# First layer from a step table, with swapped rows in its second stage; stages of the later batches moved

## The chip, the cores and the metric

The kernel runs on one NeuronCore of a Trainium2 chip. TensorE (PE) multiplies matrices into PSUM; VectorE (DVE), ScalarE (ACT) and GpSimd (POOL) work element by element, and only the first two of them read PSUM here; SyncE (SP) issues most of the DMAs, GpSimd the loads of inputs. Each engine works through its own queue in order and waits on semaphores. The metric is the device time of one execution in microseconds.

## The reference

The input `x` is 8 batches of 3008 rows and 256 columns. Each column of a batch is filtered in the frequency domain, and the result goes through two matrices with a leaky ReLU between:

```python
X = np.fft.rfft(x, axis=1)
y = np.fft.irfft(X * (filt_r + 1j * filt_i)[None], n=3008, axis=1)
h = y.reshape(24064, 256) @ w_in          # 256 x 2048
out = np.maximum(0.01 * h, h) @ w_out     # 2048 x 256
```

## The kernel before

3008 is 94 times 32, so the transform is done as two small ones in each direction, four stages of matmuls with constant tables. Stage one (s1) multiplies x by a 94-point table, stage two (s2) by one 32-point table for each of 24 columns of frequencies, then the filter is applied, stage three (sa) goes back over the 32 points and stage four (sb) over the 94. Between stages one and two, and between three and four, the data must be turned so that another index lies on the partitions.

**Batches 1 to 7** turn through DRAM. `s1_group` writes pieces of `dz1`, `t1_load` reads them back as `z1`, `s2_group` multiplies and applies the filter, `sa_group` multiplies and stores to `dz2`, `t2_load` reads `z2`, and `sb_group` makes `yt`, the input of the expert layers. Each stage has 16 or 12 groups per batch. Real and imaginary parts lie in the upper and lower 64 partitions, and the filter is complex. So `s2_group` makes two products on VectorE: p1 with `fa_sb`, which holds the real filter in both halves, and p2 with `fb_sb`, which holds the imaginary one with a changed sign in one half. Two DMAs on SP swap the halves of p2 into p3 (in batch 1 every second group writes p3 swapped, by two half-height operations), and GpSimd adds p1 and p3.

**Batch 0, the first layer,** must be done before any expert matmul and is written out by hand. `first_s1` does stage one; `t1_part` turns by VectorE's 32x32 transpose within SBUF; `first_s2` does stage two, twice 128 columns of data (`hf`), and multiplies by the two filters: on VectorE straight from PSUM, or, with `on_pool`, by a ScalarE copy and GpSimd. `first_sa` needs no swap, since it adds two matmuls, one with the table `inv2` and one with its halves exchanged, `inv2x`. `first_t2` turns again, and `first_sb` makes `yt` in 16 groups, each copied by ScalarE or VectorE (`quad_copy`). The filter is loaded to 64 partitions of `fa_sb` and `fb_sb`; `upper` fills the other 64, on ScalarE for `fa_sb`, on VectorE with the sign turned (`minus`) for `fb_sb`. `keep_warm` puts matmuls on zeros into TensorE's gaps.

**The expert layers** run over 47 chunks of 512 tokens. `moe1` multiplies by `w_in`, 16 pieces of 2 matmuls, with ScalarE's leaky ReLU for every second piece. `plain` multiplies by `w_out` directly (chunks 0 to 3 and the last). `products` does it with seven products of half size instead of eight; for these, VectorE makes sums of the activations (`act_sums`, four per chunk) and of the outputs, and `wt_sums` prepares sums of the weights.

**What orders the work.** After the first layer, everything is put into a heap with a time in *steps* and issued in that order on each engine: `at(time, f)`, or `soon(delay, f)` from inside another item. One chunk of `moe1` is 8 steps. `plan(b, s1, s1_step, s2, s2_step, lag, sb, sb_step, xl, x_step)` gives each group of batch b its time: s2 group g is at s2 + s2_step·g, its sa group `lag` later, and so on. The groups are then sorted, with at least GAP = 0.6 steps between any two. Loads are placed LANDED steps after the last group of the stage that they read, but not before `s2 - 3` or `sb - 3`:

```python
after = when[stage, b, 15 if stage == 1 else 11] + LANDED
at(max(time, after, place.get((stage, c % 4), 0)), f)
```

The step times decide only the order within each queue; on the chip an item runs when its queue reaches it and its semaphores allow.

Of the kernel before, what the change touches and what calls it, by code (L numbers as in the profile page):

```python
# [11 lines left out]
P = 128  # L12
FP16 = mybir.dt.float16
FP32 = mybir.dt.float32
# [5 lines left out]
N1, N2 = 94, 32  # L20
# [6 lines left out]
def _build_np_constants(N):  # L27
# [36 lines left out]
    inv2x = np.concatenate([inv2[64:], inv2[:64]], axis=0)  # L64
    small = np.stack([fwd1, inv2, inv2x], axis=1)
# [8 lines left out]
def kernel(  # L74
# [25 lines left out]
    LANDED = 1.7  # L100
    SUMS = (0.9, 1.9, 2.9, 3.9)
# [11 lines left out]
    small_sb = cpool.tile([P, 3, P], FP16, name="small_sb")  # L113
# [36 lines left out]

    def soon(delay, f):
        at(clock["now"] + delay, f)
# [3 lines left out]
    fwd1, inv2, inv2x = (small_sb[:, i, :] for i in range(3))  # L156
# [11 lines left out]
    def filt_load(dst, src, d0, dn):  # L168

        for q, first, sgn in ((0, 0, 1), (Q, N1, -1)):  # L170
            nc.gpsimd.dma_start(
                dst[q : q + Q, :, ds(d0, dn)],
                bass.AP(tensor=src.tensor, offset=src.offset + first * D + d0,
                        ap=[[N1 * D, N2 // 2], [sgn * NC * D, 2], [sgn * D, NC], [1, dn]]))
# [8 lines left out]
    for hf in range(2):  # L183
        filt_load(fa_sb, filt_r, hf * DH, DH)
        filt_load(fb_sb, filt_i, hf * DH, DH)
        if hf == 0:
            nc.gpsimd.dma_start(f2_sb[:, ts(2, NC // FP), :], f2_d.ap()[2])
# [26 lines left out]
    st1, st2, st1_more = ring(big[2], 0), ring(big[2], 1), ring(big[0], 0)  # L214

    def s1_group(b, g, copy):
        def go():
            ps = bank("pf", 2, D)
            nc.tensor.matmul(ps, fwd1[:N1], x_sb[:N1, ds(2 * g, 2), :], start=True, stop=True)  # L219
            h = g // 2  # L220
            st = st1[h % 4] if b > 1 or h < 4 else st1_more[h % 4]
            copy(st[:, ds(2 * (g % 2), 2), :], ps)  # L222
            if g % 2:
                soon(0.7, lambda: nc.sync.dma_start(dz1[b % 2][ds(4 * h, 4)].rearrange("n p d -> p n d"), st))
        return go

    def t1_load(b, c):
        def go():
            nc.sync.dma_start(z1[c % 4], turned(dz1[b % 2], N2, c))
        return go  # L230

    def t2_load(b, h):
        def go():
            nc.sync.dma_start(z2[h % 4][:K4], turned(dz2[b % 2], NC, h))
        return go
# [11 lines left out]
    def t1_part(b, i, flat=False):  # L247
        def go():
            a = big[(4 * b) % 3][:].bitcast(FP32)[:, ts(i, E4 * Q)].rearrange("p (e n) -> p e n", n=Q)
            o = big[(4 * b + 1) % 3][:].bitcast(FP32)  # L250
            if flat:
                o = o[:, ts(i, E4 * Q)].rearrange("p (e n) -> p e n", n=Q)
            else:
                o = o.rearrange("p (n e) -> p e n", n=Q)[:, ts(i, E4), :]
            nc.vector.transpose(o, a)
        return go


    ys = {}

    def s2_group(b, g):
        def go():
            ps = bank("pf", 2, D)
            for j in range(2):
# [8 lines left out]
            else:  # L273
                nc.vector.tensor_tensor(p2[:], ps, fb, AL.mult)  # L274
                soon(1, lambda: nc.sync.dma_start(p3[0:64], p2[64:P]))
                soon(1, lambda: nc.sync.dma_start(p3[64:P], p2[0:64]))
            nc.vector.tensor_tensor(p1[:], ps, fa, AL.mult)  # L277
            ys[(b, g)] = y1 = ypp.tile([P, 2, D], FP16, tag="y", name=f"y_b{b}_g{g}")
            soon(1.2 if b == 1 and g % 2 == EXG else 3 if b > 1 else 2.6, lambda: nc.gpsimd.tensor_tensor(y1[:], p1[:], p3[:], AL.add))  # L279
        return go  # L280

    def sa_group(b, g):
        def go():
            ps = bank("pf", 2, D)
            nc.tensor.matmul(ps, inv2, ys.pop((b, g))[:], start=True, stop=True)  # L285
            h = g // 2
            nc.scalar.copy(st2[h % 4][:, ds(2 * (g % 2), 2), :], ps)  # L287
            if g % 2:
                soon(0.7, lambda: nc.sync.dma_start(dz2[b % 2][ds(4 * h, 4)].rearrange("k p d -> p k d"), st2[h % 4]))
# [7 lines left out]
    def sb_group(b, g, copy):  # L297
        h, dt = g // 2, g % 2

        def go():  # L300
            ps = bank("pf", 4, N1)
            for j in range(4):
# [6 lines left out]
    two = ("pf", "ph")  # L309
    act, dve = nc.scalar.copy, nc.vector.tensor_copy  # L310

    def first_s1(n0, n, kind, copy):
        ps = bank(kind, n, D)
        for j in range(0, n, 2):
            nc.tensor.matmul(ps[:, ds(j, 2), :], fwd1[:N1], x_sb[:N1, ds(n0 + j, 2), :],
                             start=True, stop=True)
        spread(big[0], n0, ps, copy)
# [4 lines left out]
             for hf in range(2)]  # L322

    def first_s2(hf, c, n, kind, on_pool=False):
        ps = bank(kind, n, DH)
        src = paired(big[1])
        for j in range(n):
            nc.tensor.matmul(ps[:, j, :].rearrange("p (e t) -> p e t", t=2), f2_sb[:, c + j, :],
                             src[:, c + j, ts(hf, DH // 2)], start=True, stop=True)
        fs = [f[:, ds(c, n), ts(hf, DH)] for f in (fa_sb, fb_sb)]  # L330
        y = [prods[hf][:, i, ds(c, n), :] for i in range(2)]
        if on_pool:
            xs = [scrp.tile([P, 4, DH], FP32, tag=f"p{j // 4 + 1}", name=f"fx_h{hf}_c{c + j}")
                  for j in range(0, n, 4)]
            for j, xf in enumerate(xs):
                act(xf[:], ps[:, ts(j, 4), :])
            for i in range(2):
                for j, xf in enumerate(xs):
                    nc.gpsimd.tensor_tensor(y[i][:, ts(j, 4), :], xf[:], fs[i][:, ts(j, 4), :], AL.mult)
        else:  # L340
            for i in range(2):
                nc.vector.tensor_tensor(y[i], ps, fs[i], AL.mult)

    def first_sa(hf, c, n=4):
        y = [prods[hf][:, i, ds(c, n), :] for i in range(2)]
        for j in range(0, n, 4):
            ps = bank("pf", 4, DH)
            for i, m in enumerate((inv2, inv2x)):
                nc.tensor.matmul(ps, m, y[i][:, ds(j, 4), :], start=(i == 0), stop=(i == 1))  # L349
            act(paired(big[2])[:, ds(c + j, 4), ts(hf, DH // 2)],  # L350
                ps.rearrange("p n (t e) -> p n e t", t=2))


    def first_t2(i):
        a = big[2][:].bitcast(FP32)[:, ts(i, E4 * Q)].rearrange("p (e n r) -> p e n r", n=Q // 2, r=2)
        o = big[0][:].bitcast(FP32).rearrange("p (h n e r) -> p h e n r", h=2, n=Q // 2, r=2)
        nc.vector.transpose(o[:, i // 2, ts(i % 2, E4)], a)

    def first_sb(g, copy, kind):
        dt, h = g // 8, g % 8  # L360
        src = big[0][:].rearrange("p (h n e r t) -> p h n r t e", h=2, n=Q // 2, r=2, t=2)
        ps = bank(kind, 4, N1)
        for j in range(4):
            n2 = 4 * h + j
            for t in range(2):
                nc.tensor.matmul(ps[64 * t : 64 * t + 64, j, :], src[:, dt, n2 // 2, n2 % 2, t, :],
                                 i1_sb[:, n2, :], start=True, stop=True)
        quad_copy(h, dt, ps, copy)

    def upper(hf, t, copy):  # L370
        copy(t[64:P, :, ts(hf, DH)], t[0:64, :, ts(hf, DH)])

    def minus(o, i):
        nc.vector.tensor_scalar(o, i, -1.0, None, AL.mult)

# [6 lines left out]
    keep_warm(18)  # L382
    g = 0
    for (n0, nn), fill in zip(first_parts, (4, 3, 1, 14)):
        while nn:
            n = 2 if nn % 4 or n0 >= N2 - 4 else 4
            first_s1(n0, n, two[n // 4], (dve, act)[g % 2])
            n0, nn, g = n0 + n, nn - n, g + 1
        keep_warm(fill)
    t1_part(0, 0, True)(), t1_part(0, 1, True)()  # L390
    upper(0, fa_sb, act), upper(0, fb_sb, minus)
    first_s2(0, 8, 8, "ph", True)
    t1_part(0, 2, True)()
    first_s2(0, 0, 8, "ph")

    nc.vector.memset(i1_sb[:, 0, 0:2], 0.0)
    nc.sync.dma_start(i1_sb[:], i1_d.ap())
    first_s2(0, 16, 4, "pf", True)
    for n0 in (0, N2 // 2):
        x_load(1, n0, N2 // 2)  # L400
    t1_part(0, 3, True)()
    first_s2(0, 20, 4, "pf")
    upper(1, fa_sb, act)
    upper(1, fb_sb, minus)
    keep_warm(4)
    first_s2(1, 8, 8, "ph", True)
    first_s2(1, 0, 8, "ph")
    first_sa(0, 0, 8)
    first_s2(1, 16, 8, "ph")
    nc.gpsimd.dma_start(w_out_sb[:], moe_w_out.rearrange("(ct p) d -> p ct d", p=P))  # L410
    first_sa(0, 20), first_sa(0, 8, 8), first_sa(0, 16)
    first_sa(1, 0, 8)
    keep_warm(3)
    first_t2(0), first_t2(1)
    first_sa(1, 16), first_sa(1, 20), first_sa(1, 8, 8)
    first_t2(2), first_t2(3)
    keep_warm(2)
    for g in range(8):
        first_sb(g, act, two[(g // 2) % 2])
    for g in range(8, 16):  # L420
        first_sb(g, act if g in (10, 12, 14) else dve, two[(g // 2) % 2])
# [44 lines left out]
    def act_sums(ci, step):  # L466
# [3 lines left out]
        nc.vector.tensor_tensor(o, i0, i1, op)  # L470

# [171 lines left out]
```

## Time and profile before

| | |
|---|---|
| three runs | 756.97, 759.53, 760.03 us, median 759.53 |
| profiled execution | 758.15 us, span from the first to the last instruction 756.4 us |
| busy: PE, ACT, DVE, POOL | 740.5, 563.0, 483.1, 165.0 us |
| largest group on PE | L442 (`moe1`), 447.2 us for 1728 matmuls, which overlap |
| first expert matmul | at 38.4 us |
| HBM | 57.48 MB read, 50.33 MB written |

Line numbers are those of the kernel before. A row of the timeline or of a group reads: start, length, engine, line, operation, what it writes and reads, how often, and in brackets the idle time before it with what ended it. A chain of waits is followed back from the last instruction: start, length, what was running or awaited. "PEclk" is the clock granted to TensorE, in tenths of full speed in the page's slices and as a fraction in a table of stretches.

### The profile page before, as it was taken

The page shows a single profiled execution, that of the slowest core. Times are in us where ns is not written, and L with a number is a line of the kernel's source. Part 1 is how long each engine was busy: PE and PEld are TensorE (multiplying, and loading weights), DVE is VectorE, ACT ScalarE, POOL GpSimd, SP SyncE. Part 2 cuts the span into 40 slices and gives each one's busy share as a digit, 9 for nine tenths or more (in the row PEclk, how much of TensorE's full clock was granted, in tenths as well). Part 3 has the DMA queues.
Part 4 walks back from the last instruction along what each step waited for, and adds up shares of the span by engine and source line. Part 5 has one row for each costly group of instructions (what it writes and reads, how often), then busy time and mean ns, then how long its engine had stood idle before and what let it go on. Part 6 is the DMA issues. An engine that isn't in the chain of part 4 may idle for free.

```text
span 756.4 us, 18976 instructions
## 1 busy us (share of the span) xinstructions
PE 740.5 (98%) x7829; PEld 529.5 (70%) x7829; DVE 483.1 (64%) x658; ACT 563.0 (74%) x755; POOL 165.0 (22%) x171
## 2 busy tenths in 40 slices
PE   8899989999999999999999999999999999999998
PEld 4556657677677777877678767787777777777776
DVE  5965525777666685767667666676667766555462
ACT  4876777788778877777778777878777777776663
POOL 4703421332223121221233222212111210000000
PEclk9999999999999999999999999999999999999999
DMA  9997786887985668555665656544554433121012
GB/s 190 245 215 193 172 203 172 197 197 201 223 207 144 142 185 209 145 158 127 188 191 138 163 141 184 145 141 116 154 154 121 119 92 103 57 64 53 29 44 70
DMA packets 119687, 113.29 MB, mean 150 GB/s; under 512 B 16352, under 2 KB 92768, under 8 KB 119408
## 3 DMA queue, kind: packets, MB, share of 16 engines
q1 hardware_dynamic: 104736, 95.59, 42.8%
q0 software_dynamic: 14864, 16.49, 15.7%
q8 instruction: 61, 1.00, 0.6%
q14 instruction: 26, 0.21, 0.1%
HBM read 57.48 MB, written 50.33 MB: 143 GB/s over the span
## 4 chain that ended last, share of the span: by engine, by line
PE 88%; DMA 5%; DVE 3%; ACT 2%; issue 1%; POOL 1%; SPq 0%; DVEq 0%; POOLq 0%; ACTq 0%
PE ph L442 39%; PE pf L493 17%; PE po_ps L493 17%; PE pf L219 3%; PE pf L303 3%; PE pf L265 2%; PE pf L285 2%; DMA p_b_g<-p_b_g 2%; DMA big<-dz 2%; PE po_ps L545 1%; PE pf L545 1%; PE po_ps L379 1%; DMA dz<-big 1%; PE pf L349 1%; POOL y_b_g L279 1%
## 5 line engine op out<-in xcount | busy, mean ns | idle before, releaser
L447 ACT ACTIVATE gt_c<-ph 128x1024 f16<-128x1024 f32 x376 | 385.4, 1025 | 138.1 <-PE ph L442 129.4
L442 PE MATMUL ph<-yt,w_in_sb 128*128 128x512 f16 (+7 forms) x1728 | 447.2, 351 | 0.0
L493 PEld LDWEIGHTS <-gt_c 128*128 128x128 f16 x2688 | 194.3, 98 | 91.6 <-issue 2.8
L279 POOL TENSOR_TENSOR y_b_g<-p_b_g,p_b_g 128x512 f16<-128x512 f32 x84 | 114.0, 1358 | 443.8 <-DMA p_b_g<-p_b_g 309.5
L493 PEld LDWEIGHTS <-big 128*128 128x128 f16 x2016 | 144.8, 98 | 61.8 <-issue 1.1
L442 PEld LDWEIGHTS <-w_in_sb 128*128 128x128 f16 x1728 | 138.1, 98 | 19.7 <-issue 1.0
L274 DVE TENSOR_TENSOR p_b_g<-pf,fb_sb 128x512 f32<-128x512 f32 x78 | 53.7, 689 | 51.8 <-PE pf L265 31.5
L493 PE MATMUL pf<-wt_sb,gt_c 128*128 128x128 f16 x672 | 67.5, 219 | 0.0
L493 PE MATMUL po_ps<-wt_sb,gt_c 128*128 128x128 f16 x672 | 67.4, 219 | 0.0
L222 ACT CAST big<-pf 128x512 f16<-128x512 f32 x100 | 58.2, 583 | 11.9 <-PE pf L219 10.7
L493 PE MATMUL po_ps<-wt_sb,big 128*128 128x128 f16 x672 | 64.8, 219 | 0.0
L493 PE MATMUL pf<-wt_sb,big 128*128 128x128 f16 x672 | 64.0, 219 | 0.0
L493 PE MATMUL po_ps<-w_out_sb,gt_c 128*128 128x128 f16 x672 | 63.9, 219 | 0.0
L493 PE MATMUL pf<-w_out_sb,gt_c 128*128 128x128 f16 x672 | 63.5, 219 | 0.1
L295 ACT CAST yt<-pf 128x376 f16<-128x376 f32 x117 | 55.0, 472 | 9.5 <-PE pf L303 7.2
L277 DVE TENSOR_TENSOR p_b_g<-pf,fa_sb 128x512 f32<-128x512 f32 x84 | 57.2, 681 | 0.2
L287 ACT CAST big<-pf 128x512 f16<-128x512 f32 x84 | 49.1, 584 | 9.6 <-PE pf L285 8.4
L470 DVE TENSOR_TENSOR gt_c<-gt_c 128x2048 f16<-128x2048 f16 x42 | 54.5, 1297 | 1.1
L470 DVE TENSOR_TENSOR big<-gt_c,big 128x2048 f16<-128x2048 f16 x42 | 54.9, 1308 | 0.0
L470 DVE TENSOR_TENSOR big<-big,gt_c 128x2048 f16<-128x2048 f16 x42 | 52.7, 1256 | 0.0
L470 DVE TENSOR_TENSOR big<-gt_c 128x2048 f16<-128x2048 f16 x42 | 52.1, 1241 | 0.2 <-ACT gt_c L447 0.2
L219 PE MATMUL pf<-x_sb,small_sb 94*128 94x512 f16 x112 | 42.7, 381 | 1.1 <-DVE p_b_g L277 0.9
(84 smaller groups left out, 642.4 us busy)
## 6 DMA issues: line engine op xcount, KB each, us to landing
dz<-big SPq DMA_DIRECT2D x98, 256.0 KB
p_b_g<-p_b_g SPq DMA_DIRECT2D x156, 128.0 KB
out_dram<-ost_c_h SPq DMA_DIRECT2D x114, 128.0 KB
big<-dz SPq DMA_DIRECT2D x42, 256.0 KB
big<-dz SPq DMA_DIRECT2D x56, 192.0 KB
x_sb<-in_x_dram POOLq DMA_DIRECT2D x41, 192.0 KB, 4.5
out_dram<-ost_c_t SPq DMA_DIRECT2D x14, 128.0 KB
x_sb<-in_x_dram POOLq DMA_DIRECT2D x2, 768.0 KB, 10.1
```

The source lines that it names most:

```text
L219: nc.tensor.matmul(ps, fwd1[:N1], x_sb[:N1, ds(2 * g, 2), :], start=True, stop=True)
L222: copy(st[:, ds(2 * (g % 2), 2), :], ps)
L274: nc.vector.tensor_tensor(p2[:], ps, fb, AL.mult)
L277: nc.vector.tensor_tensor(p1[:], ps, fa, AL.mult)
L279: soon(1.2 if b == 1 and g % 2 == EXG else 3 if b > 1 else 2.6, lambda: nc.gpsimd.tensor_tensor(y1[:], p1[:], p3[:], AL.add))
L287: nc.scalar.copy(st2[h % 4][:, ds(2 * (g % 2), 2), :], ps)
L295: copy(yv, ps.rearrange("p c a -> p a c"))
L303: nc.tensor.matmul(ps[:, j, :], z2[h % 4][:K4, j, ts(dt, P)], i1_sb[:K4, 4 * h + j, :], start=True, stop=True)
L442: nc.tensor.matmul(ph[:, j, ds(t - ci * CH, e - t)], w_in_sb[:, dt, ts(ct, P)], yt[:, dt, ds(t % N, e - t)], start=(dt == 0), stop=(dt == ...
L447: nc.scalar.activation(gts[ci][:, ds(2 * g, 2), :], ph, AF.Lrelu)
L470: nc.vector.tensor_tensor(o, i0, i1, op)
L493: nc.tensor.matmul(po[:, t], a()[:, c, ts(t, P)], w[:, c, :], start=(c == 0), stop=(c == NCH - 1))
```

## The change

*One filter tensor at first.* The loads put the real filter into partitions 0 to 63 of `fa_sb` and the imaginary one into 64 to 127; `upper` and `minus` are gone. Stage two of the first layer is done twice: once as before (`i` = 0), once with the two 64-column halves of its table exchanged (`i` = 1), each half with a matmul of its own, so that real and imaginary rows come out swapped. Each result is multiplied by the same `fa_sb`, and two new tables `inv2r` and `inv2i` in stage three add what belongs together.

*A table.* The first layer is a list of steps, `FIRST`, each with its PSUM bank and engine; matmuls, copies and products are separate steps. Transposes write a layout in which stage two's moving operand takes 4 bytes in every 8; before, it took 4 in every 128.

*Two token groups.* Of the second half's eight sb groups only (1,1) and (1,0) are in the table. The other six are issued at steps REST among the expert layers (`late_sb`).

*Filter copies later.* At steps 1 to 5, two SBUF-to-SBUF DMAs on SP and two sign changes on VectorE fill `fb_sb` and the lower half of `fa_sb` for the other batches.

*Stages moved.* All numbers of `plan`, LANDED, SUMS and the delays of `soon` are new; the planner now defers a group whose load or sum would not yet have been issued; `need` only asserts an order when the kernel is built.

```diff
-    inv2x = np.concatenate([inv2[64:], inv2[:64]], axis=0)
-    small = np.stack([fwd1, inv2, inv2x], axis=1)
+    inv2r = np.concatenate([inv2[:64], -inv2[:64]], axis=0)
+    inv2i = np.concatenate([inv2[64:], inv2[64:]], axis=0)
+    small = np.stack([fwd1, inv2, inv2r, inv2i], axis=1)
...
-    LANDED = 1.7
-    SUMS = (0.9, 1.9, 2.9, 3.9)
+    LANDED = 2.25
+    SUMS = (0.05, 1.56, 2.78, 3.96)
+    REST = (7.03, 10.88, 12.69, 11.1, 24.89, 21.68)
+    DUE = (3.63, 2.43)
+    LEAD = (3.88, 6.11)
+    AFTER = (0.93, 0.81, 2.51, 2.97, 0.07, 0.45)
+    PLANS = (
+        (0.68, 0.1, 11.58, 1.11, 3.68, 36.48, 2.65, 7.08, 1.57),
+        (11.42, 1.71, 43.13, 2.47, 7.03, 86.57, 2.71, 17.89, 2.06),
+        (39.96, 1.77, 73.73, 3.9, 5.24, 128.81, 2.92, -0.44, 2.56),
+        (64.08, 2.86, 119, 3.89, 7.18, 177.38, 3.01, 9.84, 2.43),
+    )
...
-        filt_load(fa_sb, filt_r, hf * DH, DH)
-        filt_load(fb_sb, filt_i, hf * DH, DH)
+        filt_load(0, filt_r, hf * DH, DH)
+        filt_load(64, filt_i, hf * DH, DH)
...
+            for h in range(2):
+                nc.tensor.matmul(ps[ts(h, 64), j, :].rearrange("p (e t) -> p e t", t=2),
+                                 f2_sb[:, c + j, ts(1 - h, 64)], v, start=True, stop=True)
...
+        s1e 0 12 4 A, s1e 0 24 2 D, s1p 0 20 4 b3, s1e 0 20 4 A, s1p 0 26 2 b0, s1p 0 28 2 b1,
+        s1p 0 30 2 b2, s1e 0 26 2 D, s1e 0 28 2 A, s1e 0 30 2 D, t1 1, t1 0, warm 14, s2p 0 0 4 0 b0,
+        s2p 0 0 4 1 b1, s2p 0 16 4 0 b2, t1 2, t1 3, s2a 0 0 4 0, s2m 0 0 4 0, s2a 0 0 4 1, s2p 0 16 4 1 b0,
...
+        sbp 0 0 b2, sbp 0 3 b4, sbe 0 6 A, sbp 1 1 b3, sbe 0 0 D, sbe 0 2 A, sbp 1 0 b0, sbe 0 3 A,
+        sbe 0 7 A, sbe 1 1 D, sbe 1 0 A
...
+    for g in range(10, 16):
+        at(REST[g - 10], lambda g=g: late_sb(1, g - 8, (act, dve)[g % 2]))
...
-    plan(1, 0.3, 0.55, 12.8, 1.25, 3.3, 37, 2.8, 4, 1.6)
-    plan(2, 13, 1.55, 43.5, 2.6, 5.5, 84.2, 2.8, 13, 2.3)
-    plan(3, 42, 1.75, 75, 3.75, 6, 129, 2.94, 4, 2.94)
-    for b in range(4, B):
-        z = 47 * b
-        plan(b, z - 121, 2.94, z - 69, 3.92, 6.5, z - 11.6, 2.94, 4, 2.94)
+    at(1, lambda: nc.sync.dma_start(fb_sb[0:64], fa_sb[64:P]))
+    for i in range(2):
+        at(1 + i, lambda i=i: nc.vector.tensor_scalar(fb_sb[64:P, ts(i, NC // 2)], fa_sb[64:P, ts(i, NC // 2)],
+                                                      -1.0, None, AL.mult))
+    at(5, lambda: nc.sync.dma_start(fa_sb[64:P], fa_sb[0:64]))
```

In the table, `s1p`, `s2p`, `sap` and `sbp` are the matmuls of a stage, `s1e`, `sae` and `sbe` the copies out of PSUM (A on ScalarE, D on VectorE), `s2d` a product on VectorE, `s2a` with `s2m` a ScalarE copy with a product on GpSimd, `t1` and `t2` the transposes, `warm` the filler.

## The prediction

> **What bounds the kernel now.** I read the page first: busy shares, then the forty slices.
>
> ```profile
> span 756.4 us, 18976 instructions
> ...
> PE 740.5 (98%) x7829; PEld 529.5 (70%) x7829; DVE 483.1 (64%) x658; ACT 563.0 (74%) x755; POOL 165.0 (22%) x171
> ...
> PE   8899989999999999999999999999999999999998
> ...
> PEclk9999999999999999999999999999999999999999
> ```
>
> TensorE is busy all the way, so time can be won in two places only: ahead of the first expert matmul, where a busy PE proves little (part of it is `keep_warm` filler), and in single PE stalls later. The chain of waits supports this: 88% of it is PE, 39% L442 alone. So next the timeline of VectorE in the first layer:
>
> ```profile
> 14.78 2.37 DVE L255 STREAM_TRANSPOSE big<-big 128x1024 f32<-128x1024 f32 x2 [0.22 <-ACT big L243]
> 17.18 0.95 DVE L374 TENSOR_SCALAR fb_sb<-fb_sb 64x3072 f16<-64x3072 f16 x1
> ...
> 33.51 2.37 DVE L357 STREAM_TRANSPOSE big<-big 128x1024 f32<-128x1024 f32 x2 [1.03 <-ACT big L350]
> 36.50 1.00 DVE L295 CAST yt<-pf 128x376 f16<-128x376 f32 x2 [0.61 <-PE pf L366]
> ```
>
> From 14.78 to 35.88 (33.51+2.37) VectorE rests once, 1.03 us before the last transposes, because ScalarE came late. VectorE sets the first layer's end; the first expert matmul (L442) starts at 38.4. The stretches show that PE has slack there:
>
> ```profile
> 20.68:24.10 3.42, 1.41 (x13) 1.22 (x13) 3.39 (x6) 2.35 (x2) 3.42 (x4) 1.00 1.25 216
> 24.10:27.50 3.40, 3.40 (x20) 2.10 (x18) 3.37 (x3) 2.22 (x4) 3.39 (x5) 0.50 1.03 286
> ```
>
> (columns: length, then PE, PEld, DVE, ACT, POOL busy, PE clock, DMA share, GB/s). PE is busy 1.41 of 3.42 us while VectorE has 3.39; in the next stretch PE's clock is half.
>
> For the rest I listed the places where one PE matmul starts later than its predecessor's length allows. From 38.4 to 753 only these exceed 0.3 us: 57.4 (0.73), 68.7 (0.37), 74.2 (0.33), 110.8 (2.11), 142.7 (1.11), 192.8 (0.83), 366.3 (1.90), 452.2 (1.22): 8.6 us. The chain at two of them, cut out:
>
> ```profile
> 52.27 2.60 DMA dz<-big
> ...
> 55.07 3.15 DMA big<-dz
> ...
> 58.27 0.38 PE pf L265 x2
> ```
>
> At 57.4 batch 1's second stage waits for the turn through DRAM: store 2.60, load 3.15. At 110.8 it is the second turn (4.85 and 2.94). At 192.8, 366.3 and 452.2 a swap or load took 6.23, 5.89 and 6.91; at 142.7 a VectorE sum stood in front.
>
> [...] 16 first-layer matmuls of 128 columns (L328), whose moving operand takes 4 bytes in every 128, last 1.92 us, 0.11 each; L493's 128 columns, contiguous, go at 0.39/7=0.056. That 4 bytes in every 8 run at full speed, no row shows. [...] L366's 64-column pairs agree: groups of 16 start at 32.97 and 33.47, 0.50/8=0.06 per pair.
>
> **The change, part by part.** Baseline: span 756.4; that execution timed 758.15, the three timed runs 756.97 to 760.03, median 759.53. I carry the difference over to the median.
>
> *First layer, VectorE.* First stage: the three 1024-element casts of 1.22 become two, with three of 0.68; the last cast (DVE or ACT) ends at 14.28 instead of 14.75: −0.5. The two sign flips (0.95+1.37) leave the path: −2.3. Products: GpSimd took ten of 512 elements (about 1.15 each), now eight; VectorE now has six of 1024 at 1.21 and four of 512 at 0.66, 9.9, against 8.56 in its eight rows before: +1.3. The transposes keep their number and about 1.19 each (L357 has the new output pattern already). The 1.03 rest goes, since ScalarE loses two copies of 2.75 (L371) and takes eight of 0.54 (five before): its last copy before the final transposes comes about 0.3 ahead of them. VectorE's row is then 14.3 + 8×1.19 + 9.9 + 0.06 = 33.8 against 35.88: −2.1. After it, only the two groups (1,0) and (1,1) stand before the first expert matmul instead of eight: their copies, two of 0.54 on VectorE and ScalarE's last ones ending at 35.5, let PE run from about 35.4, 1.6 behind the transposes against 2.5. Sum: **−3.0**.
>
> This needs PE to keep up. Swapped rows add 96 matmuls of 64 columns, in 48 pairs. At 0.056–0.06 each both halves take 96×0.058=5.6 against 48×0.11=5.3; at 0.11 they take 10.6, PE becomes the row that sets the end, and walking it step by step puts the first expert matmul at 37.6–38.0: the gain shrinks to −0.6. [...]
>
> *Moved out.* Six sb groups (`late_sb`) cost PE 0.25 each among full work: **+1.5**. Their copies go to ACT and DVE, which have room (5 to 6 tenths busy).
>
> *Filter copies.* Two SBUF copies on SP and two sign flips on VectorE come back at steps 1 to 5. SP holds its copies behind the filter loads' landings (22.0) and the table load only; the dz1 stores queue behind them. The first flip (0.95) stands on VectorE between two evacuations that PE's stage-one groups need back: **+0.8** (0 to 1.2). The copies' 1.5 MB meet w_out and x: 219 to 271 GB/s there before. The inverse table `i1` is issued at 21.5 (21.7 before, landed 30.09) and needed at 31.4: 0 to +0.7, taken as 0. On GpSimd's queue the loads of batch 1's x and of w_out stand two products earlier, about 3 us ahead of 26.4 and 31.9: they land sooner, nothing waits. The next table, f2, still waits for the last second-stage matmul, at about 27.
>
> *Batch 1's first turn.* LANDED and AFTER put the z1 loads at step 12.88 instead of 11.0. On SP they now stand behind chunk 0's second output store (`t1`), which waits for a VectorE copy that ended at 56.5 before; load at about 57.1, landing 60.3, against PE ready at 57.7 (its group is at 12.91 instead of 12.8). A stall of 2.1 to 2.6 in place of 0.73: **+1.4**. Behind the store on SP wait only those loads and the swaps that follow them; behind the stalled group on PE waits everything, so it counts in full. Bounds: 0.7 (nothing changes) to 3.4, if stores and loads take 0.7 longer.
>
> *Plans.* One step is about 1.85 us here. Last sa to first sb in batch 1: 3.6 → 4.3 steps, −1.2 of the 2.11 at 110.8. Batch 1's sa lags: −0.4. The sums leave step 0.9 for 0.05, away from the product that they delayed at 142.7: −1.0. Batch 2's group 11 gets 5.4 steps instead of 4.8 (+1.1 us): −0.8. Batch 4's group 11 gets 6.24 instead of 6.04 (+0.4) and its swap is queued 0.19 steps earlier: −1.2 of 1.90, the softest term. Batch 6's loads lead by 4.16 instead of 3.0 (+2.1): −1.2. Batch 3's sa groups lose: 4.1 to 6.0 steps instead of 5.0 to 6.65. Measured from s2 to the end of GpSimd's add, its chains took 5.8 to 10.5 us; four of twelve exceed the new lag, by about 2 us less what overlaps: +0.8. Sum: **−5.0**.
>
> Total −3.0+1.5+0.8+1.4−5.0 = −4.3: span 752.1, and 759.53−4.3 = **755.2**.
>
> **Rivals.**
> A (0.56): the sum above; 755.2, own range 751.5–758.5.
> B (0.18), stage two stays at half rate: −0.6 for −3.0, so 757.6. [...]
> C (0.16), the later stalls are jitter of DMAs (3.15 here, 6.91 there) that no plan removes: the −5.0 shrinks to 0, 760.2. For it: batch 4's groups have equal lags, and one of twelve stalled. Against: the stalled groups of batches 1, 2 and 6 had the shortest lags.
> D (0.10), slower: batch 3's second stage, 190 to 280 us, becomes a rhythm of waits: s2, swap, add, sa. Its twelve lags average 5.2 steps. Two neighbouring groups overlap, so a chain of c steps costs about 12(c−5.2)/2 steps. At 8.2 us over A, from chains of about 5.9 steps (11 us), the kernel is slower than before beyond 0.5%; at 12.3 us it ends at 771. For it: 10.0, 10.0 and 10.5 in three groups now. Against: a median of 7.6.
> That the change doesn't do what it says: the filter is loaded with the same bytes and its two other halves are made later, so no transfer is saved, only its place moves; included in A.
>
> **How the numbers follow.** Measurement can tell about 0.5%, 3.8 us, from no change: below 755.7 is faster, above 763.3 slower. A's value lies close under the first bound, and what it may err in (the bounds above) reaches more to the low side, since its losses can be smaller and no stall may remain: 0.48 of its 0.56 I count as faster, with 0.04 of B and 0.02 of C: 0.54. D gives 0.10 slower; 0.36 stays. Low end of the range: A without the flip's 0.8, the turn's 1.4, batch 3's 0.8, and with the rest of the 1.90 and 2.11 won: 755.2−3.0−1.6 = 750.6, put at 750.0. High end: C with the table's 0.7, 761.0; D lies outside.
>
> **What would show it.** Right: VectorE without rest from 14.3 to about 33.8; first L501 matmul near 35; PE clock full from 7 on; L385 rows at about 0.056 per matmul; a PE wait of 2 us on big<-dz near 57; none at 110, 366, 452. Wrong: L385 at 0.11; PE clock halves in several stretches; waits for the add at many groups between 190 and 280; a first L501 later than 37.

## The result, and the profile after

The change made the kernel slower: 766.31 us median of six runs (765.88 to 771.32) against 756.99 (756.16 to 760.03) of the kernel before, ratio 1.0132 with a 95% interval of 1.0096 to 1.0169. The prediction was 755.2, with a range of 750 to 761. The profiled execution of the kernel after timed 766.39.

The page of the kernel after, the lines that answer to those of before:

```profile
span 764.6 us, 19178 instructions
...
PE 742.4 (97%) x7920; PEld 528.9 (69%) x7920; DVE 486.9 (64%) x660; ACT 560.1 (73%) x757; POOL 167.1 (22%) x169
...
PE   8968999999999999999999999999999999999997
...
PEclk9989999999999999999999999999999999999999
```

PE has one slice of 6 tenths, the third (38 to 57 us), with a clock of 8: the loss lies right behind the first layer. Line numbers from here on are those of the kernel after: L501 is `moe1`, L607 `plain`, L247, L296, L318 and L339 the four stages' matmuls, L250 the copy behind L247, L430 the first layer's sb groups, L252 the dz1 stores, L259 the z1 loads, L542 the output stores.

VectorE in the first layer, from the timeline:

```profile
14.39 4.62 DVE L376 STREAM_TRANSPOSE big<-big 128x1024 f32<-128x1024 f32 x4
19.69 2.36 DVE L393 TENSOR_TENSOR prod<-ph,fa_sb 128x1024 f16<-128x1024 f32 x2 [0.67 <-PE ph L385]
...
29.14 4.81 DVE L422 STREAM_TRANSPOSE big<-big 128x1024 f32<-128x1024 f32 x4
33.87 0.51 DVE L329 CAST yt<-pf 128x376 f16<-128x376 f32 x1
```

From 14.39 to 33.95 VectorE rests once, for 0.67 us, and the first L501 starts at 35.17 (38.44 before). The first layer does what was forecast. What PE waited for next, from 34 to 58 us and from 58 to 70:

```profile
PE po_ps L607 <- DMA w_out_sb<-in_moe_w_out_dram: 6.0, 1, 6.0
PE pf L247 <- DVE big L250: 0.8, 1, 0.8
...
PE pf L296 <- DMA big<-dz: 2.7, 1, 2.7
```

(columns: us in total, times, longest). The first `plain` waits 6.0 us for `w_out`, a load that the kernel before had in time. Its issue, from GpSimd's timeline before, and issue to landing, from the chain after:

```profile
31.94 1.22 POOL L410 DMA_DIRECT2D w_out_sb<-in_moe_w_out_dram  x1
```

```profile
28.48 24.61 DMA w_out_sb<-in_moe_w_out_dram
```

Before, the load took 12.6 us and landed at 44.5. The stretches from the wait on:

```profile
46.74:53.12 6.38, 0.38 (x2) 0.10 (x1) 0.68 (x1) 0.90 (x1) 0.00 (x0) 0.79 1.25 255
53.12:57.33 4.21, 4.21 (x15) 2.16 (x15) 0.69 (x1) 1.02 (x1) 0.00 (x0) 0.51 0.96 251
```

PE has 0.38 busy in 6.38, then runs 4.21 us at a clock of 0.51, in which about 2.1 us are lost: the wait of 6.0 costs about 8. A rest of 2.0 us in the kernel before (20.9 to 22.9) has half clock behind it too (0.50 from 24.1 to 27.5). After the 2.7 at the second wait here (65.9 to 68.6) the clock stays full (1.00 from 65.9 to 73), as it does behind a rest of 1.9 in the kernel before (1.00 from 111 to 117). So in these traces the length of a rest alone doesn't tell whether half clock follows. The chain at the second wait:

```profile
63.69 0.43 DVE ost_c_t L612
64.12 0.02 issue
64.14 0.58 SPq L542
...
64.94 3.54 DMA big<-dz
68.48 0.14 issue
68.61 0.38 PE pf L296 x2
```

The z1 loads are issued only after chunk 0's output store (L542), which waited for VectorE's copy of PSUM (L612).

**A ledger.** For every matmul in the trace I took the time to the next one's start and subtracted its own length (0.213 us for 512 columns, as four of L501 at full clock go from start to start: 1.02 us at 35.17, the last one 0.38); the rest is called excess. Before against after: first expert matmul 38.4 to 35.2, −3.3. Matmul work after it 683.0 to 684.9, +1.9 (`late_sb`). Excess up to 58 us 1.2 to 9.7, +8.5; from 58 to 70 us 0.6 to 3.6, +3.0 (of the 1.2, 0.73 is the wait at batch 1's first turn, which the kernel after has behind 58 us; like against like it is +9.2 and +2.3); from 70 to 195 us 8.6 to 7.5, −1.1; from there to the end 20.7 to 19.3, −1.4. Behind the last matmul 3.9 to 4.5, +0.6. The sum is +8.2, the difference of the spans of the two profiled executions; the medians differ by 9.3.

### The profile page after: what moved, and what is told of

The parts are those of the page before. It is cut to its first block, busy times and chain, and to the rows that moved or that the text cites. A ratio compares the mean times of both kernels' runs of the same rounds, so it can differ in the third digit from the quotient of the medians.

```text
span 764.6 us, 19178 instructions
## 1 busy us (share of the span) xinstructions
PE 742.4 (97%) x7920; PEld 528.9 (69%) x7920; DVE 486.9 (64%) x660; ACT 560.1 (73%) x757; POOL 167.1 (22%) x169
## 3 DMA queue, kind: packets, MB, share of 16 engines
q8 instruction: 62, 1.02, 0.6%
## 4 chain that ended last, share of the span: by engine, by line
PE 85%; DMA 10%; POOL 2%; DVE 2%; issue 1%; SPq 0%; ACT 0%; DVEq 0%; POOLq 0%; ACTq 0%
PE ph L501 39%; PE pf L555 17%; PE po_ps L555 17%; DMA w_out_sb<-in_moe_w_out_dram 3%; PE pf L339 3%; PE pf L247 2%; DMA p_b_g<-p_b_g 2%; PE pf L296 2%; PE pf L318 2%; DMA f_sb<-fwd_const 1%; PE po_ps L607 1%; PE pf L607 1%; POOL y_b_g L311 1%; DMA big<-dz 1%; DMA x_sb<-in_x_dram 1%
## 5 line engine op out<-in xcount | busy, mean ns | idle before, releaser
L501 PE MATMUL ph<-yt,w_in_sb 128*128 128x512 f16 (+7 forms) x1728 | 448.2, 352 | 0.5 <-DVE yt L329 0.5
L555 PEld LDWEIGHTS <-gt_c 128*128 128x128 f16 x2688 | 194.6, 98 | 89.1 <-issue 1.1
L311 POOL TENSOR_TENSOR y_b_g<-p_b_g,p_b_g 128x512 f16<-128x512 f32 x84 | 118.1, 1408 | 428.1 <-DMA p_b_g<-p_b_g 307.9
L501 PEld LDWEIGHTS <-w_in_sb 128*128 128x128 f16 x1728 | 137.8, 98 | 22.7 <-issue 3.2
L250 ACT CAST big<-pf 128x512 f16<-128x512 f32 x100 | 58.1, 583 | 12.9 <-PE pf L247 11.1
L529 DVE TENSOR_TENSOR gt_c<-gt_c 128x2048 f16<-128x2048 f16 x42 | 58.0, 1382 | 0.9
L607 PEld LDWEIGHTS <-gt_c 128*128 128x128 f16 x320 | 31.4, 99 | 25.8 <-issue 8.3
```

Source lines behind the costliest of these rows:

```text
L311: ("y", b, g), lambda: nc.gpsimd.tensor_tensor(y1[:], p1[:], p3[:], AL.add)))
L501: nc.tensor.matmul(ph[:, j, ds(t - ci * CH, e - t)], w_in_sb[:, dt, ts(ct, P)], yt[:, dt, ds(t % N, e - t)], start=(dt == 0), stop=(dt == ...
L555: nc.tensor.matmul(po[:, t], a()[:, c, ts(t, P)], w[:, c, :], start=(c == 0), stop=(c == NCH - 1))
L607: nc.tensor.matmul(po, gts[ci][:, ct, ts(tj, P)], w_out_sb[:, ct, :], start=(ct == 0), stop=(ct == NCT - 1))
```

## The experiments

All times are medians of the compared runs; each group of kernels had its own runs of the kernel before (757.18 for the first four kernels, 756.76 for the next four, 756.68 for the last two). The first four take apart what the ledger shows between 35 and 70 us, and the moved stages.

**Filter copies on VectorE instead of by DMA.**

```diff
-    at(1, lambda: nc.sync.dma_start(fb_sb[0:64], fa_sb[64:P]))
+    for i in range(2):
+        at(3 + i, lambda i=i: nc.vector.tensor_copy(fb_sb[0:64, ts(i, NC // 2)], fa_sb[64:P, ts(i, NC // 2)]))
...
-    at(5, lambda: nc.sync.dma_start(fa_sb[64:P], fa_sb[0:64]))
+    for i in range(2):
+        at(5 + i, lambda i=i: nc.vector.tensor_copy(fa_sb[64:P, ts(i, NC // 2)], fa_sb[0:64, ts(i, NC // 2)]))
```

> The changed kernel with its two filter DMAs replaced by four VectorE copies of 64x3072 at steps 3 to 6 (about 0.95 us each, as the sign flips). Theory T: the first filter copy's 12 KB packets held the DMA engines from 37 to 42 us and pushed the w_out load into the time of the dz1 stores; without them w_out lands at 44 to 46 us instead of 53.1, the 6.2 us wait before the first L607 and the half clock after it (about 2.1 us) go, and the kernel takes 757 to 759.5 us (0.988 of the changed kernel, at most 1.5 us given back for the new VectorE copies). Rival R1: w_out is late because the table queues it behind batch 1's x and starts the dz1 stores at 39 us; then it lands after 50 us and the wait stays above 3 us, the kernel above 762.

Measured: 759.37, 7 us under the kernel after. `w_out` landed 17.2 us after its issue at 29.0, at 46.2, hardly later than expected, and no PE wait for it is left. Its waits from 34 to 54 us:

```profile
PE pf L247 <- DVE big L250: 2.1, 4, 0.8
PE pf L430 <- DVE big L250: 0.9, 1, 0.9
```

So theory T holds, and the new VectorE copies cost about 2 us of PE, where at most 1.5 was expected: each, 0.95 us long, stands in front of a copy that frees a PSUM bank.

**The two DMAs later.**

```diff
-    at(1, lambda: nc.sync.dma_start(fb_sb[0:64], fa_sb[64:P]))
+    at(9.5, lambda: nc.sync.dma_start(fb_sb[0:64], fa_sb[64:P]))
...
-    at(5, lambda: nc.sync.dma_start(fa_sb[64:P], fa_sb[0:64]))
+    at(9.6, lambda: nc.sync.dma_start(fa_sb[64:P], fa_sb[0:64]))
```

> The changed kernel with the two filter DMAs at steps 9.5 and 9.6 instead of 1 and 5, nothing else moved. Theory T: w_out lands at 44 to 46 us, no wait before L607; the 1.5 MB of the copies now meet the dz1 stores and z1 loads instead, which delays the first second-stage group of batch 1 by up to 3 us; 758 to 761 us. Rival R1: w_out after 50 us, wait above 3 us, 764 or more.

Measured: 763.34, between the two expectations. `w_out` took 16.6 us and nobody waits for it, as T says, but the price at the other place was far too small. The waits from 34 to 70 us:

```profile
PE pf L296 <- DMA big<-dz: 7.7, 1, 7.7
PE pf L247 <- DVE big L250: 0.8, 1, 0.8
```

The chain at that wait, cut:

```profile
56.60 5.54 DMA dz<-big
...
62.22 2.96 DMA big<-dz
```

The last dz1 store now stands on SP behind both copies and took 5.54 us, the z1 loads came after it, and the wait is 7.7 us instead of 2.7. The second copy overwrites what the first one reads, and SP waited 5.3 us for that: it was issued at 55.0, a microsecond after the first one's last packets, and its packets fill 56 to 60 us; the store's come after them. So this place moves the wait. It doesn't show that no place would do: from 54 to 56 us the DMA engines moved nothing.

**The step numbers of before, on the kernel with VectorE copies (the first one).**

```diff
-    LANDED = 2.25
-    SUMS = (0.05, 1.56, 2.78, 3.96)
+    LANDED = 1.0
+    SUMS = (0.9, 1.9, 2.9, 3.9)
...
-    AFTER = (0.93, 0.81, 2.51, 2.97, 0.07, 0.45)
+    AFTER = (0.7, 1, 3, 2.6, 0.7, 0.5)
...
-        (0.68, 0.1, 11.58, 1.11, 3.68, 36.48, 2.65, 7.08, 1.57),
+        (0.3, 0.55, 12.8, 1.25, 3.3, 37, 2.8, 4, 1.6),
```

(DUE, LEAD and the other three plans likewise; the 1.0 is added to a delay of 0.7.)

> As the kernel with VectorE filter copies, but all step numbers of the stages (plans, sums, landing time, delays) as before the change. Theory P (the moved stages gain, as the prediction summed: about 5.0 us less the first turn's 1.4): slower than the kernel with VectorE copies by 2 to 4.5 us, with stalls again at batch 1's first sb group, at a product behind a VectorE sum, and at the groups 11. Rival C (those stalls are chance of single DMAs): within 1 us of it, stalls of the same total at other groups.

Measured: 758.76, 0.6 us faster than with the new numbers. Theory P's loss didn't come. The time lies within rival C's 1 us, but not for C's reason: the stalls are back at three of P's places (1.19 at batch 1's first sb group, 1.04 behind a VectorE sum at 146, 0.93 at batch 2's group 11), and excess from 70 to 195 us is 9.7 instead of 7.6. What pays for them is seen in the next kernel: in the old numbers batch 1's z1 loads stand ahead of the second output store.

**z1 loads ahead of the store.**

```diff
-            at(t, (t1_load if stage == 1 else t2_load)(b, c))
+            at(t - 0.6 * (stage == b == 1 and c < 4), (t1_load if stage == 1 else t2_load)(b, c))
```

> As the kernel with VectorE filter copies, but batch 1's first four z1 loads stand ahead of chunk 0's second output store on SP; nothing else moves on any queue. Theory Z: the loads start about 1 to 2 us earlier, and the stall before batch 1's first second-stage group, which stands at about 2 to 3 us, shrinks to under 1.2 us; 1.5 to 2.5 us faster than with the VectorE copies alone. Rival: the dz1 stores land too late anyway, the loads start within 0.4 us of before, and the time is the same within 0.5 us.

Measured: 756.04, 3.3 us under the same kernel without it. Theory Z holds and was too low: the wait of 3.1 us became 0.2, and the half clock behind it (64.4 to 67.8 us) went too. The chain to L296 without the change and with it, cut; in the second the waiting DMA is gone:

```profile
58.97 0.55 SPq L542
...
59.75 3.73 DMA big<-dz
63.48 0.14 issue
63.61 0.38 PE pf L296 x2
```

```profile
59.84 0.32 PE po_ps L607 x2
60.16 0.04 issue
60.20 0.38 PE pf L296 x2
60.58 0.43 PE ph L501 x2
```

With this order alike on both sides, the old step numbers (758.76) are 2.7 us slower than the new ones (756.04). So the moved stages are worth −2.7, and the place of one load in SP's queue +3.3: together +0.6.

**Copies and flips in small pieces.** Two kernels, on the one above. In the first all 24 pieces are VectorE's, in the second GpSimd's, at steps 0.1, 0.4 and 0.7 + 1.1·i; the lines that they replace are left out:

```diff
...
+    for i in range(8):
+        w = ts(i, NC // 8)
+        at(1.1 + 1.2 * i, lambda w=w: nc.vector.tensor_scalar(fb_sb[64:P, w], fa_sb[64:P, w], -1.0, None, AL.mult))
+        at(1.5 + 1.2 * i, lambda w=w: nc.vector.tensor_copy(fb_sb[0:64, w], fa_sb[64:P, w]))
+        at(1.9 + 1.2 * i, lambda w=w: nc.vector.tensor_copy(fa_sb[64:P, w], fa_sb[0:64, w]))
```

> As the kernel with VectorE filter copies and z1 loads ahead of the store, but the six filter operations of 64x3072 (0.95 us each) cut into 24 of 64x768 spread over steps 1 to 11. Theory V: the PE waits of 0.98, 0.70, 0.77, 1.03 and 0.35 us between 37 and 48 us come from single long VectorE operations that stand in front of the copies that free the PSUM banks; cut, they fall to under 1.2 us together and the kernel takes 753 to 754.5 us. Rival: VectorE is short of time as a whole there, and the waits keep a sum above 2.5 us: 755.5 to 756.5 us.

Measured: 755.92, no gain; the rival's number. Excess from 35 to 50 us is 3.2 us instead of 4.1. A piece of a quarter took 0.35 us instead of 0.95/4 = 0.24, so the cutting added 24×0.35 − 6×0.95 = 2.7 us of VectorE time: this run doesn't separate length from sum.

> As the last, with the 24 pieces on GpSimd, which has nothing to do between 31 and 58 us. Theory V: no PE wait between 37 and 57 us but the first second-stage group; 752.5 to 754 us. Rival: GpSimd needs over 1 us for each piece of 64x768 and batch 1's second stage waits for the filter, or GpSimd's pieces lengthen VectorE's copies: 756 us or more.

Measured: 766.08, the rival's side. GpSimd's timeline:

```profile
30.09 2.15 POOL L639 TENSOR_SCALAR fb_sb<-fa_sb 64x768 f16<-64x768 f16 x1
32.30 0.82 POOL L640 COPY fb_sb<-fa_sb 64x768 f16<-64x768 f16 x1
...
61.24 0.82 POOL L641 COPY fa_sb<-fa_sb 64x768 f16<-64x768 f16 x1
62.02 1.10 POOL L188 DMA_DIRECT2D x_sb<-in_x_dram  x2
```

A copy takes 0.82, a sign flip 2.15; the filter is ready at 62.1. But PE doesn't wait for the filter first:

```profile
PE pf L247 <- DMA x_sb<-in_x_dram: 11.5, 1, 11.5
```

L247 is stage one of batch 2. Its x is loaded by GpSimd, whose queue reaches these loads (L188) only behind the last piece. The time was the rival's, its cause was not. From 35 to 50 us excess is 0.7: with VectorE free, PE hardly waits there. That led to the last version: copies on GpSimd, flips on VectorE.

**The six late groups early again,** on the kernel with the z1 loads ahead:

```diff
-    REST = (7.03, 10.88, 12.69, 11.1, 24.89, 21.68)
+    REST = (-0.6, -0.5, -0.4, -0.3, -0.2, -0.1)
```

> As the kernel with VectorE filter copies and z1 loads ahead of the store, but the six late token groups stand ahead of the first expert matmul, as all eight did before the change. Theory F (the prediction's accounting: their 48 matmuls cost PE the same 1.9 us of work in either place, but early PE also waits for the bank copies): the first L501 moves from 35.1 to 37.3 to 38.5 us, the kernel is 0.3 to 1.5 us slower. Rival: since PE waits in 37 to 48 us anyway, the six groups ahead give those waits away and the time is the same or up to 1 us faster.

Measured: 757.17, 1.1 us slower (1.6 if each is set against its own group's kernel before), at or just above theory F's range. The first L501 is at 39.75, later than F said: PE waits about 2 us for bank copies between those groups (0.44, 0.77, 0.51, 0.36), and from 38.9 to 42.3 us the clock is half.

**Batch 1's first sb groups 0.6 steps later.**

```diff
-            groups.append((min(sb + sb_step * g, due - DUE[0] + DUE[1] * (g % 2)), 4, b, g, sb_group(b, g, act)))
+            groups.append((min(sb + sb_step * g, due - DUE[0] + DUE[1] * (g % 2)) + 0.6 * (b == 1 and g < 2), 4, b, g, sb_group(b, g, act)))
```

> As the kernel with VectorE filter copies and z1 loads ahead of the store, but batch 1's first two sb groups 0.6 steps (1.1 us) later. Theory L (the wait of 1.8 us at batch 1's first sb group is a lag too short for the turn through DRAM): it falls to 0.6 to 1.0 us and the kernel is 0.8 to 1.1 us faster. Rival: another wait follows at the second pair of groups or at the chunk that needs them, and the time is the same within 0.4 us.

Measured: 755.27, 0.8 us faster, 0.4 if each is set against its own group's kernel before; the 95% intervals of the two ratios overlap (0.9965 to 0.9988 and 0.9955 to 0.9981), so the gain isn't clear of noise. The wait fell from 1.81 to 0.66, as theory L says.

**All that helped.**

```diff
...
+    for i in range(8):
+        w = ts(i, NC // 8)
+        at(0.5 + 0.8 * i, lambda w=w: nc.vector.tensor_scalar(fb_sb[64:P, w], fa_sb[64:P, w], -1.0, None, AL.mult))
+        at(0.1 * i, lambda w=w: nc.gpsimd.tensor_copy(fb_sb[0:64, w], fa_sb[64:P, w]))
+        at(0.9 + 0.8 * i, lambda w=w: nc.gpsimd.tensor_copy(fa_sb[64:P, w], fa_sb[0:64, w]))
```

> The changed kernel with everything that has helped: 16 copies of 64x768 on GpSimd (0.82 us each, 13 us in all, done near 44 us), 8 sign flips of 64x768 on VectorE (0.36 each), z1 loads ahead of the store, batch 1's first two sb groups 0.6 steps later. Theory V (long VectorE work in front of the copies that free banks is what PE waits for between 37 and 48 us): the excess of PE there falls from 4.1 to under 1.7 us and the kernel takes 752 to 753.5 us, 0.4 to 0.6% under the kernel before. Rival: [...] VectorE's pieces grow longer, the excess stays above 3 us: 755 us.

Measured: 752.65 against 756.68, ratio 0.9943 (0.9924 to 0.9962): faster than both kernels. PE's waits from 34 to 70 us:

```profile
PE pf L247 <- DVE big L250: 0.6, 2, 0.4
PE po_ps L607 <- DMA w_out_sb<-in_moe_w_out_dram: 0.5, 1, 0.5
PE ph L501 <- DVE yt L329: 0.5, 1, 0.5
```

Excess from 35 to 50 us is 1.95, a little above what was expected. Since the copies left VectorE and the flips were cut at once, length and sum of VectorE's work aren't separated here either.

**The copies alone, put into the kernel before.**

```diff
+    at(1, lambda: nc.sync.dma_start(fa_sb[64:P], fa_sb[0:64]))
+    at(5, lambda: nc.sync.dma_start(fa_sb[64:P], fa_sb[0:64]))
```

> The kernel before with two DMAs of 768 KB added, fa_sb's upper half over its lower one with the same values, at steps 1 and 5 on SP, as the changed kernel has its filter copies; nothing else. Theory T (the copies alone delay w_out and the turn): w_out lands at 48 to 53 us instead of 44.5, its first user L545 waits 0 to 4 us, batch 1's first second-stage group waits 3 to 7 us instead of 0.7; 4 to 9 us slower than before in all. Rival R1 (the table's order does it, the copies are harmless): within 1.5 us of before.

Measured: 766.09 against 756.68, +9.4, ratio 1.0124 (1.0103 to 1.0144). The chain in it (L545 is `plain` there, L265 the second stage):

```profile
32.39 20.18 DMA w_out_sb<-in_moe_w_out_dram
52.57 0.04 issue
52.61 0.37 PE po_ps L545
...
57.55 5.68 DMA dz<-big
...
63.30 3.08 DMA big<-dz
66.39 0.04 issue
66.43 0.59 PE pf L265 x2
```

Nothing else of the change is in this kernel, and it shows both waits: 3.3 us for `w_out`, 3.6 at the turn. So the copies are enough to make the loss; the table's order isn't needed for it. The loss was a little above the range given, since half clock follows both waits: a pair of L442 takes 0.85 us at 54.05 and at 67.23, and 0.43 at 55.93 and 69.34. The profiled execution, 768.97, was the slowest of the six.

## Why the prediction was wrong

- **Filter copies: the step that failed.** The text named the transfers ("The copies' 1.5 MB meet w_out and x") and priced them at nothing: the loads on GpSimd's queue "land sooner, nothing waits". Only the flip was counted, at 0.8, and it cost 0.98. `w_out` was issued 3.5 us earlier (28.5 instead of 31.9) and landed 8.6 us later (53.1 instead of 44.5). In the trace's DMA records, w_out's 512-byte packets all but stop where the first copy's come: from 38 to 40 us, 30 packets of 12,288 bytes on SP's queue, 0.96 us each, and 28 of 512 bytes on GpSimd's, 0.06 us each. So about as many packets start on the one queue as on the other, and this leaves `w_out` 14 KB in 2 us where it moved 374 KB (748 packets) in the kernel before. From 42 us on it shares with the dz1 stores (1469 packets of w_out's and 942 of 512 bytes on SP's queue from 42 to 48 us), and at the end with the second copy, whose packets come from 50.9 on: from w_out's last packet (51.7) to its landing it took 1.4 us, 0.3 before. Nor would it have landed sooner without the copies: in the three kernels where none is in its way (copies on VectorE, copies late, z1 loads ahead) it was issued at 28.4 to 29.0 and landed at 45.0 to 46.2. Its packets start at 37.0 to 37.1 there and at 37.6 before, as those of batch 1's x, ahead of it on GpSimd's queue, end. It could have been read ahead: in the kernel before, the DMA share is 1.25 and 1.03 in the two stretches that the prediction shows and 1.34 from 38.4 to 46 us, and `w_out` landed only 4.4 us ahead of its first user at 48.9. The prediction took the rate for room. The sum is 6.2 for the wait, 2.1 for the half clock and 1.0 for the flip: +9.2 instead of +0.8.
- **Batch 1's first turn.** Mechanism right, size small: a wait of 2.9 us in place of 0.73 (2.1 to 2.6 was said), +2.2 instead of +1.4. The planner puts loads and group at steps 12.86 and 12.89, not 12.88 and 12.91, which changes nothing. With the copies on VectorE the order on SP is worth 3.3 us, since there half clock follows the wait of 3.1; in the kernel after, the clock stayed full.
- **First layer.** Right: −3.3 for −3.0, first L501 at 35.17 (35.4 said). L385 goes at 0.058 us from start to start, so the second stage doesn't run at half rate and rival B falls. (The prediction's full rate was its author's estimate; no row of before showed it.) A pair of L389 takes 0.59/8 = 0.074, above the 0.06 taken. VectorE's rest didn't go; it is 0.67 at 19.0, where PE waited 0.78 for a table.
- **Moved out.** Too small: +1.9 by the ledger's lengths for +1.5, and from the end of the matmul ahead to the start of the next one a group takes 0.47 to 0.71, 3.1 for six. The groups early again were 1.1 us slower, so `late_sb` pays.
- **Plans.** −5.0 was said, −2.7 measured between the two kernels that differ in the step numbers and have the z1 order alike. Batch 1's part failed: −1.2 and −0.4 were said. The wait at its first sb group stayed (1.95 after, 2.11 before): the turn took 9.2 us in the kernel with the z1 loads ahead, store 4.82 and load 4.33, instead of 7.8, so the added lag was eaten; and its last sa group now waits 0.89. Batch 2's group 11 waits no more (0.83 before), as said. The wait of 0.77 at 207.4 stands one sa group later in PE's order, at batch 3's first, whose lag went from 5.0 to 4.2 steps: the loss that the text put at 0.8. The sum at 142 went as said. The waits of batches 4 and 6 are gone, but they are gone with the old step numbers behind the new first layer as well, while the kernel before with copies has the one of 1.90 again (at 377.7); and a wait of 1.13 at 392.2 in the kernel after is in none of the eight other kernels with its numbers. Their 2.4 us in the sum were not the plan's to win for certain, so on this part rival C's number was nearer; its reason, chance of single DMAs, isn't shown, since the 1.90 stands alike in both kernels with the old first layer.
- **Rival D** falls: from 195 to 300 us excess is 4.0 us (3.4 before), with one wait of 0.77, at batch 3's first group. The loss came from a place that no rival named.

What of w_out's delay is the size of the copies' packets, and what their bytes, wasn't separated. Nor was it tried to load `w_out` ahead of batch 1's x.

## What to carry to other kernels

Here two copies between places of SBUF cost as transfers do: in the kernel before, `w_out` took 12.6 us, and 20.2 with the copies put in. Before such a copy is priced at nothing, list what is in flight on the DMA engines from its issue to the first user of each load, with each load's slack. Where a step moves in an in-order queue, look at the instruction that it now stands behind and at what that one waits for; a wait on TensorE can cost more than its length: here half clock followed the waits of 3.1 us (copies on VectorE), 3.3 and 3.6 (before with copies), 6.0 (after) and 7.7 (copies late), and one rest of 2.0 (before), but not those of 1.9 (before) and 2.7 (after). A gain booked on single waits of one execution isn't safe until a second execution shows the same waits.

## What was not expected of the hardware

An add of GpSimd lasts 1.27 us as a rule (11 of the 84 before took over 1.5), and 2.23 in front of the wait at 366.3. The timelines of VectorE and GpSimd in the kernel before, at that place:

```profile
365.88 1.23 DVE L470 TENSOR_TENSOR big<-gt_c 128x2048 f16<-128x2048 f16 x1
367.14 2.17 DVE L470 TENSOR_TENSOR gt_c<-gt_c 128x2048 f16<-128x2048 f16 x1
```

```profile
366.00 2.23 POOL L279 TENSOR_TENSOR y_b_g<-p_b_g,p_b_g 128x512 f16<-128x512 f32 x1 [12.50 <-DVE ost_c_h L525]
```

The add starts 0.12 behind a VectorE sum and ends 1.12 after it; the next sum starts in the meantime, lasts 2.17 instead of 1.23, and ends 1.09 after the add. In the whole kernel before, each of the 11 adds over 1.5 us began while a sum of L470 ran, and each of the 13 sums over 1.5 us (of 168) while an add ran. So either lasts longer where it began beside the other; why isn't shown. With the old step numbers behind the new first layer, the add was over at 369.21, before the sum at 369.26, and no wait followed. That this order decides over the 1.90 is likely, not shown: other things moved there too. And GpSimd's sign flip of 64x768 takes 2.15 us where its plain copy takes 0.82 and VectorE's flip 0.36.
